# Who issues the last part of the first gate weights: SyncE in place of ScalarE, in an S5 scan with a gated GLU

## The chip, the cores and the metric

The kernel runs on one core of a Trainium2 chip. The metric is device time in microseconds (us), the median of several runs of the whole program; lower is better. A core has five engines with an instruction stream each: PE (TensorE, matmuls; PEld is its weight load), DVE (VectorE), ACT (ScalarE), POOL (GpSimd) and SP (SyncE, which here only issues DMAs). DMAs can be issued by SP, by ACT and by POOL.

## The reference, cut to what matters

```python
def _A_ref(x, Lambda_re, Lambda_im, B_re, B_im, C_re, C_im, log_dt, Dskip):
    ...
    for t in range(L):
        h = Lam_bar[None, :] * h + Bu[:, t, :]
        hs.append(h)
    hseq = jnp.stack(hs, 1)
    y = 2.0 * jnp.einsum("blp,dp->bld", hseq, Cmat).real + x * Dskip[None, None, :]
    return y

def _B_ref(x, w_gate, w_up, w_down):
    g = jnp.einsum("bsd,df->bsf", x, w_gate)
    u = jnp.einsum("bsd,df->bsf", x, w_up)
    h = _sigmoid(g) * u
    return jnp.einsum("bsf,fd->bsd", h, w_down)

x = A_x                                   # 1 x 2048 x 448, bfloat16
xn = _layernorm(x, axis=-1)
s = _A_ref(xn, ...)                       # 448 complex states
g = _silu(_B_ref(xn, B_w_gate, B_w_up, B_w_down))   # w_gate, w_up: 448 x 1792
return x + s * g
```

So every token is normalized once; the normalized token feeds a gated feed-forward block (gate, up, down) and a diagonal complex recurrence over time, and the two meet at the end.

## The kernel before, in words

The 2048 tokens are 16 tiles of 128 (tile t is rows 128t to 128t+127), and four chunks of 512 tokens. Everything that PE reads has tokens along the free axis, so a tile is normalized first and then transposed into `xnT`. Chunk 0 is transposed on PE, the later chunks by DMA.

**The order of the work** is not written out by hand engine by engine. Each step is given to a planner (`Plan`, lines 74 to 243) with an estimated cost, its reads (`r=`) and its writes (`w=`); a DMA also has a rate and, in the head of the kernel, an expected landing time (`land=`). The planner computes due times backward and a schedule forward, and the instructions are then emitted in the order of the planned starts. PE's order is fixed by a chain; DVE's and ACT's are fixed by a chain up to line 1147 and free behind it. The planner's reads order its own schedule; on the chip an instruction waits only for semaphores of work that it really depends on, and a DMA also for the landing of the DMA that used the same semaphore before it (there are eight, in turn, for the DMAs of SP and ACT together).

**The head**, up to the first dense matmul, goes like this.

- Lines 403 to 406: tile 0 is loaded by SP, tile 1 by ACT, tile 2 by SP and tile 3 by ACT, 112 KB each. Line 407: a row of parameters, by SP.
- Lines 409 to 412, `load_w0`: the first block of the gate weights (two column groups of 128, for the lower half of the hidden axis on partitions 0 to 63 and for the upper half on partitions 64 to 127), in four parts. Part A of the lower half (96 KB) by SP, part A of the upper half (128 KB) by ACT, part B of the lower half (128 KB) by SP, part B of the upper half (96 KB) by ACT.
- Lines 419 to 438: the rest of the gate weights (block 2 of 224 KB for each half, block 3 of 336 KB for each half), tiles 4 to 7, the up weights and the skip vector, all by SP, one after the other.
- Ahead of the real work PE runs ten matmuls on constants (line 444).
- Statistics of tile 0 are DVE's (line 450 `bn_stats`, line 456 `bn_aggr`), those of tile 1 are ACT's: a mean (line 488, `act_mean`), then a variance (line 492), then a root (line 496). The roots of tiles 0, 2 and 3 are ACT's too (line 484). DVE takes the reciprocals (line 481) and normalizes (line 530).
- PE transposes tile 0 (lines 568 and 570) in two groups; ACT copies the second group of slots first (line 578, "b"), then the first ("a"). Tiles 1, 2 and 3 are transposed once (lines 588, 589), copied by ACT (line 592) and shifted by DVE (line 599).
- The first two gate steps run tile by tile on PE (lines 827 and 828, function `last_tile`): for tile 0 the "b" slots, which read only parts A of the weights, then the "a" slots, which read parts B as well; then tiles 1, 2, 3. Line 827 takes the lower half of the weights, line 828 the upper half.
- From then on PE runs full 512-token steps (lines 809 and 810), first the other gate steps of chunk 0, then the seven up steps, then the projection into the states (`b_phase`, lines 883 to 900), and so on chunk by chunk to the down projections (line 1025) and the outputs (line 1044).

ACT issues its DMAs from its own instruction stream, in order with its arithmetic: what stands behind a DMA issue on ACT waits until the issue is done. Before the change, ACT's stream begins: load tile 1, load tile 3, load an activation table, issue part A of the upper half, issue part B of the upper half, `act_mean(1)`, the root of tile 0, and so on.

Of the kernel before, what the change touches and what calls it, by code (L numbers as in the profile page):

```python
# [14 lines left out]
ACT = mybir.ActivationFunctionType  # L15
# [5 lines left out]
P = 128  # L21
H = 64
# [224 lines left out]
def kernel(  # L247
# [37 lines left out]
    wsrc = {"g": B_w_gate, "u": B_w_up}  # L285
# [69 lines left out]
    def load(eng, key, nbytes, o, i, cost=0.45, r=(), rate=230e3, land=0.0):  # L355
        e = {"SP": Q, "ACT": A, "POOL": G}[eng]
        add(eng, cost, lambda: e.dma_start(out=o, in_=i), w=[key] if not isinstance(key, list) else key,  # L357
            r=r, dma=nbytes, chain=True, rate=rate).land = land
# [12 lines left out]
             wgt[k][ps, :, m0 * P:m1 * P],  # L371
             wsrc[k][:, c0 + m0 * P:c0 + m1 * P].rearrange("(s p) f -> p s f", p=H), cost=0.65, r=r, rate=rate, land=land)

    def load_w0(eng, half, part, land=0.0):
        ps = slice(half * H, half * H + H)
        s0, c0 = (1 - half if part == "A" else half), half * 896
        n = 4 - s0
        load(eng, [("w", "g", half, m, part) for m in range(2)], H * n * 2 * P * 2, wgt["g"][ps, s0:7:2, 0:2 * P],
             wsrc["g"][:, c0:c0 + 2 * P].rearrange("(s p) f -> p s f", p=H)[:, s0:7:2, :], cost=0.5, rate=400e3, land=land)

    def wkeys(k, m, part=None):
        if k == "u" or m > 1:
# [18 lines left out]
    def load_p(eng, k, r=()):  # L401
        load(eng, ("vrow", k), D * 2, vrow[k:k + 1, :], (A_log_dt, A_Lambda_im, A_Lambda_re)[k].unsqueeze(0), cost=0.75 if eng == "POOL" else 0.45, r=r)
# [4 lines left out]
    load_p("SP", 2)  # L407
    add("ACT", 0.05, lambda: A.preload_act_table_set("sqrt_and_others"), w=["sqrttab"], lat=1.3, chain=True)
    load_w0("SP", 0, "A", land=5.7)
    load_w0("ACT", 1, "A", land=5.9)  # L410
    load_w0("SP", 0, "B", land=6.9)
    load_w0("ACT", 1, "B", land=6.9)
    load_p("POOL", 0)
    load_p("POOL", 1)
    add("POOL", 0.15, lambda: G.memset(ident[:], 0.0), w=["ident"], chain=True)
# [846 lines left out]
```

## Time and profile before

| | |
|---|---|
| median of the runs | 183.85 us (3 runs: 183.84, 183.85, 184.04) |
| the profiled execution's own time | 183.57 us |
| its span, first to last instruction | 181.8 us |
| what lies around the span | 1.77 us |
| granted TensorE clock, mean by the profile's record | 1.0 |
| PE / DVE / ACT / POOL busy | 177.2 / 166.3 / 97.7 / 37.3 us |
| moved by DMA | 13.43 MB |

All times in the views are in us from the start of the span. A row of the timeline has the start, the length, the engine (SPq and ACTq are the instruction streams of SP and ACT issuing a DMA), the line in the kernel, the operation, what it writes and reads, and the count of instructions merged into the row; in brackets stands the idle time of the engine before it and what ended it. A row of the chain of waits has the start, the length and the instruction that held up the end of the kernel in this stretch. A row of the DMA issues has the size of one DMA and the time from its issue to its landing.

### The profile page before, as it was taken

The page shows a single profiled execution, that of the slowest core. Times are in us where ns is not written, and L with a number is a line of the kernel's source. Part 1 is how long each engine was busy: PE and PEld are TensorE (multiplying, and loading weights), DVE is VectorE, ACT ScalarE, POOL GpSimd, SP SyncE. Part 2 cuts the span into 40 slices and gives each one's busy share as a digit, 9 for nine tenths or more (in the row PEclk, how much of TensorE's full clock was granted, in tenths as well). Part 3 has the DMA queues.
Part 4 walks back from the last instruction along what each step waited for, and adds up shares of the span by engine and source line. Part 5 has one row for each costly group of instructions (what it writes and reads, how often), then busy time and mean ns, then how long its engine had stood idle before and what let it go on. Part 6 is the DMA issues. An engine that isn't in the chain of part 4 may idle for free.

```text
span 181.8 us, 3617 instructions
## 1 busy us (share of the span) xinstructions
PE 177.2 (97%) x1404; PEld 88.4 (49%) x1411; DVE 166.3 (91%) x295; ACT 97.7 (54%) x162; POOL 37.3 (21%) x93
## 2 busy tenths in 40 slices
PE   8999999999999999999999999999999999999993
PEld 2664445564544444445554444454555444455552
DVE  2738899999999999999999999999999999999772
ACT  4899997958799983364145543348210533411101
POOL 6352437200028998000004100000000000000000
PEclk9999999999999999999999999999999999999999
DMA  4999999999000390000004900001000000001121
GB/s 144 238 219 220 189 165 178 300 189 252 22 0 0 62 143 0 0 4 0 0 2 82 149 0 0 4 0 62 14 4 0 27 25 26 3 0 63 45 78 48
DMA packets 29956, 13.43 MB, mean 74 GB/s; under 512 B 19441, under 2 KB 29938, under 8 KB 29938
## 3 DMA queue, kind: packets, MB, share of 16 engines
q1 hardware_dynamic: 29106, 12.74, 35.0%
q10 hardware_dynamic: 768, 0.46, 1.0%
q8 instruction: 11, 0.18, 0.4%
q14 instruction: 7, 0.06, 0.1%
q0 software_dynamic: 64, 0.00, 0.0%
HBM read 6.77 MB, written 1.84 MB: 47 GB/s over the span
## 4 chain that ended last, share of the span: by engine, by line
PE 94%; DMA 1%; ACT 1%; DVE 1%; issue 1%; ACTq 0%; DVEq 0%
PE gu L809 43%; PE gu L1025 15%; PE acc L1044 11%; PE acc L1025 9%; PE gu L897 8%; PE gu L883 2%; PE acc L900 2%; PE gu L827 2%; DMA x_all<-in_A_x_dram 1%; PE acc L809 1%; PE gu L810 1%; DVE o_t L1086 0%; PE gu L828 0%; ACT junk L492 0%; ACTq L357 0%
## 5 line engine op out<-in xcount | busy, mean ns | idle before, releaser
L809 PE MATMUL gu<-xnT,wU 64*128 64x512 bf16 x196 | 45.8, 377 | 0.0
L810 PE MATMUL gu<-xnT,wU 64*128 64x512 bf16 x196 | 45.8, 376 | 0.0
L810 PE MATMUL gu<-xnT,wG 64*128 64x512 bf16 (+1 forms) x189 | 41.3, 361 | 0.0
L809 PE MATMUL gu<-xnT,wG 64*128 64x512 bf16 (+1 forms) x189 | 41.3, 361 | 0.0
L843 ACT ACTIVATE sig<-gu 128x1024 f32<-128x1024 f32 x21 | 21.3, 1021 | 25.6 <-PE gu L810 18.9
L1025 PEld LDWEIGHTS <-hF 128*128 128x128 bf16 x224 | 21.9, 98 | 20.6
L809 PEld LDWEIGHTS <-wU 64*128 64x128 bf16 x196 | 18.5, 94 | 22.8
L809 PEld LDWEIGHTS <-wG 64*128 64x128 bf16 x196 | 18.5, 94 | 19.8
L1025 PE MATMUL gu<-wd,hF 128*128 128x448 bf16 x140 | 28.0, 353 | 0.0
L846 DVE SCALAR_TENSOR_TENSOR hF<-sig,gu 128x1024 bf16<-128x1024 f32 x21 | 25.4, 1207 | 0.3
L1044 PE MATMUL acc<-cT,hT 128*128 128x448 bf16 (+2 forms) x119 | 22.9, 337 | 0.0
L964 DVE TENSOR_TENSOR_SCAN wv<-c_r,st,z 128x512 bf16<-128x512 f32 x18 | 22.9, 1275 | 0.0
L1031 ACT ACTIVATE g_t<-gu 128x448 bf16<-128x448 f32 x10 | 5.4, 539 | 27.7 <-PE gu L1025 16.8
L810 PEld LDWEIGHTS <-wU 64*128 64x128 bf16 x196 | 18.5, 94 | 0.0
L810 PEld LDWEIGHTS <-wG 64*128 64x128 bf16 x196 | 18.5, 94 | 0.0
L1025 PE MATMUL acc<-wd,hF 128*128 128x448 bf16 x84 | 16.9, 353 | 0.0
L1044 PEld LDWEIGHTS <-hT 128*128 128x128 bf16 x126 | 11.6, 98 | 9.9 <-issue 0.4
L897 PE MATMUL gu<-xnT,bT 128*128 128x512 bf16 x65 | 15.3, 380 | 0.4
L911 ACT CAST bus<-gu 128x1024 bf16<-128x1024 f32 x12 | 12.0, 1010 | 5.8 <-PE gu L883 5.3
L540 POOL COPY xn<-xn 128x448 bf16<-128x448 bf16 x12 | 7.4, 629 | 31.4 <-ACT xn L534 31.2
L917 ACT CAST bus<-acc 64x256 bf16<-64x256 f32 (+1 forms) x24 | 8.7, 368 | 5.3 <-PE acc L900 4.9
L450 DVE BATCH_NORM_STATS2 bst<-x_all 128x6 f32<-128x448 bf16 x11 | 6.4, 616 | 4.7 <-DMA x_all<-in_A_x_dram 4.7
(162 smaller groups left out, 265.6 us busy)
## 6 DMA issues: line engine op xcount, KB each, us to landing
wd<-in_B_w_down_dram SPq DMA_DIRECT2D x2, 784.0 KB, 7.5
out_dram<-o_t SPq DMA_DIRECT2D x12, 112.0 KB, 1.7
wU<-in_B_w_up_dram SPq DMA_DIRECT2D x2, 448.0 KB, 11.7
x_all<-in_A_x_dram SPq DMA_DIRECT2D x2, 448.0 KB, 4.7
wG<-in_B_w_gate_dram SPq DMA_DIRECT2D x2, 336.0 KB, 5.8
wU<-in_B_w_up_dram SPq DMA_DIRECT2D x2, 336.0 KB, 8.8
wG<-in_B_w_gate_dram SPq DMA_DIRECT2D x2, 224.0 KB, 4.7
x_all<-in_A_x_dram SPq DMA_DIRECT2D x2, 224.0 KB, 8.5
```

Source lines behind the costliest of these rows:

```text
L450: add("DVE", 0.56 if t < TPC else 0.6, lambda: V.bn_stats(out=bst[b][:], in_=x_all[:, t, :]), r=[("x", t)] + ([("xnT", 0, 3, "a")] if 3 < ...
L540: add("POOL", 0.25 if n == H else 0.6, lambda: G.tensor_copy(out=o[:, D:D + n], in_=o[:, 0:n]), r=[("xn", b)], w=[("xnw", b)])
L809: T.matmul(bank[0][:, ts], lhsT=w_[0:H, s, ms], rhs=x[0:H, SL[s], ts], start=(s == 0), stop=(s == 6))
L810: T.matmul(bank[1][:, ts], lhsT=w_[H:P, (s + 1) % 7, ms], rhs=x[H:P, SL[s], ts], start=(s == 0), stop=(s == 6))
L843: add("ACT", act(1024), lambda: A.activation(th, gu[a][:], ACT.Tanh, scale=0.5), r=[("gu", a)], w=[tk])
L846: add("DVE", dve1(1024), lambda: V.scalar_tensor_tensor(out=ho, in0=th, scalar=1.0, in1=gu[a][:], op0=ALU.add, op1=ALU.mult), r=[("gu", a) ...
L897: T.matmul(gu[slots[pt]][:, i, :], lhsT=bT[:, kt, i, pt * P:pt * P + P], rhs=x[:, kt, :], start=(first and kt == 0), stop=(not first and k ...
L911: add("ACT", act(1024), lambda: A.copy(out=bus[u][:], in_=gu[slots[pt]][:]), r=key(pt), w=[("bus", u)])
L917: add("ACT", 0.36, lambda ns=ns, d=d, q=q, l=l, i=i: A.copy(out=bus[u][d, l, ns], in_=acc[a3[i]][q, 0:256]), r=[("acc", a3[i])] + ([("bus" ...
L964: dve(1.194, lambda k=k: V.tensor_tensor_scan(out=wv[:, k, :], data0=rb, data1=z[:, k, :], initial=(st[pt][:, k, :] if c else 0.0), op0=AL ...
L1025: T.matmul(d, lhsT=hF[c % 2][:, m, h, js], rhs=wd[:, ft, :], start=(ft == 0), stop=(ft == FT - 1))
L1044: T.matmul(y, lhsT=hT[c % 2][:, hm, js], rhs=cT[:, cm, c0:c1], start=(i == 0 and not skip_on_pe), stop=(i == 6))
```

## The change

Part B of the upper half of the first gate block is issued by SP instead of ACT. `load_w0` gets a parameter `r`, passed on to `load`, and the call names tile 1's load as a read.

```diff
-    def load_w0(eng, half, part, land=0.0):
+    def load_w0(eng, half, part, r=(), land=0.0):
         ps = slice(half * H, half * H + H)
         s0, c0 = (1 - half if part == "A" else half), half * 896
         n = 4 - s0
         load(eng, [("w", "g", half, m, part) for m in range(2)], H * n * 2 * P * 2, wgt["g"][ps, s0:7:2, 0:2 * P],
-             wsrc["g"][:, c0:c0 + 2 * P].rearrange("(s p) f -> p s f", p=H)[:, s0:7:2, :], cost=0.5, rate=400e3, land=land)
+             wsrc["g"][:, c0:c0 + 2 * P].rearrange("(s p) f -> p s f", p=H)[:, s0:7:2, :], cost=0.5, r=r, rate=400e3, land=land)
...
     load_w0("SP", 0, "B", land=6.9)
-    load_w0("ACT", 1, "B", land=6.9)
+    load_w0("SP", 1, "B", r=[("x", 1)], land=6.9)
```

In the built program this DMA stands on SP right behind part B of the lower half and ahead of block 2 (line 419), and every later DMA of SP stands one place further back. It keeps the same one of the eight DMA semaphores, the one of tile 1's load, and so waits for that landing, as it did on ACT. On ACT `act_mean(1)` now follows part A directly, and carries the wait for tile 1's landing itself. PE's order stays as it was. The planner, which solves everything anew, also moves instructions on the other engines from about 17 us on: on DVE the evacuation of the second up step goes ahead of the reciprocal and the mean product of tiles 6 and 7 (lines 512, 513); on ACT the normalizations of tiles 6 and 7 (line 534) go behind one more sine table (line 686), one half of an evacuation (line 840) goes ahead of a normalization, and another sine table goes some instructions back; on POOL the copy for tile 6 (line 540) goes behind one copy of the projection weights (line 748). Around 45 to 70 us some scan, scale and statistics instructions of DVE, ACT and POOL change places with their neighbours.

## The prediction

> **What bounds the kernel now.** First the page: its span, the busy times and the shares of the chain that ended last.
>
> ```profile
> span 181.8 us, 3617 instructions
> PE 177.2 (97%) x1404; PEld 88.4 (49%) x1411; DVE 166.3 (91%) x295; ACT 97.7 (54%) x162; POOL 37.3 (21%) x93
> PE 94%; DMA 1%; ACT 1%; DVE 1%; issue 1%; ACTq 0%; DVEq 0%
> ```
>
> PE is busy for 97% of the span and carries 94% of the chain; all other engines and DMAs together hold a few per cent. So a change counts if it lets PE start its real work earlier, or makes PE wait later. Second, who PE waits for (the view of waits, PE alone):
>
> ```profile
> PE gu L444 <- PEq L1246: 0.8, 1, 0.8
> PE acc L568 <- DVE g_t L530: 0.3, 1, 0.3
> ```
>
> There are two idle stretches, both before 5.5 us. From then on PE runs on to the tail, so what the head gains or loses is handed on one for one, if no later input comes too late for an earlier PE. Third, the chain of waits in the head:
>
> ```profile
> 0.73 2.54 DMA x_all<-in_A_x_dram
> 3.27 0.02 issue
> 3.29 0.60 ACTq L357
> 3.90 0.05 issue
> 3.94 0.07 ACT junk L488
> ...
> 5.78 0.19 ACT sdb L484
> 5.96 0.39 ACT xnT L578
> 6.35 0.04 issue
> 6.40 0.21 PE gu L827
> ```
>
> Tile 1 lands at 3.27, and then ACT issues the very DMA that is moved, for 0.60 us, before its mean of tile 1 starts at 3.94. This issue is on the path.
>
> **The change, part by part.** (1) *ACT loses one issue.* The mean can start at about 3.30, 0.64 earlier. What is late next is seen in the rows of ACT, DVE and PE:
>
> ```profile
> 3.94 0.58 ACT L488 ACTIVATE junk<-x_all 128x448 bf16<-128x448 bf16 x1 [1.00 <-DMA x_all<-in_A_x_dram]
> 4.52 0.28 ACT L484 ACTIVATE sdb<-mvf,epsc 128x1 bf16<-128x1 f32 x1
> 3.79 0.18 DVE L456 BATCH_NORM_AGGREGATE mvf<-bst 128x2 f32<-128x6 f32 x1
> 3.90 0.63 DVE L450 BATCH_NORM_STATS2 bst<-x_all 128x6 f32<-128x448 bf16 x1
> 4.83 0.16 DVE L481 RECIPROCAL rsd<-sdb 128x1 f32<-128x1 bf16 x1 [0.31 <-ACT sdb L484]
> 13.35 1.16 DVE L450 BATCH_NORM_STATS2 bst<-x_all 128x6 f32<-128x448 bf16 x2 [1.53 <-DMA x_all<-in_A_x_dram]
> 0.77 4.43 PE L444 MATMUL gu<-const-bfloat16-1.0 128*128 128x512 bf16 x10 [0.77 <-PEq L1246]
> 5.49 0.51 PE L568 MATMUL acc<-ident,g_t 128*128 128x128 bf16 x6 [0.29 <-DVE g_t L530]
> ```
>
> The root of tile 0 stands behind the mean on ACT (4.52). Earlier, it meets its other input: DVE's aggregate ends at 3.97, so it starts at about 4.05 and ends at 4.33. DVE is in the statistics of tile 2 by then (from 3.90, when that tile lands). Two such instructions in a row take 1.16, so 0.53 from start to start, and the reciprocal can follow at 3.90 + 0.53 = 4.43 instead of 4.83. Behind it the aggregate of tile 2 needs those statistics (end 4.53), and the normalization follows at about 4.66 instead of 5.04. **Head: 0.38**, not 0.64. PE could take its first transposes at 5.11 instead of 5.49; its ten constant matmuls don't stop it (0.77 + 10 x 0.43 = 5.07). ACT's variance, roots and copies all hang on the same starts, so the first copy goes from 5.87 to 5.49, and the gate step from 6.40 to 6.02.
>
> (2) *PE's rate at that time.* The constant matmuls take 0.43 us each for 512 columns. Later steps take 0.22, which two rows of the up steps show:
>
> ```profile
> 22.68 0.38 PE L810 MATMUL gu<-xnT,wU 64*128 64x512 bf16 x1
> 22.89 0.38 PE L810 MATMUL gu<-xnT,wU 64*128 64x512 bf16 x1
> ```
>
> So PE runs at half rate up to some moment between its last constant matmul and 5.49, where six transposes take 0.51 with the end of the last. At half rate a transpose of 128 columns costs 0.43/4 = 0.11 instead of 0.05. If the rate rises no earlier than before, the transposes that now begin at 5.11 run slow, and the first copy, which waits for three, comes about 3 x 0.055 = 0.16 later than counted. Bounds: 0 (the rate rises before 5.11) and 0.2 or more (it rises later). I take 0.16, since 5.49 is the first time at which a row shows the full rate. Head left: 0.22.
>
> The Trainium skill says in "TensorE: Matmul & The Clock Gate", Part 1, that PE runs at half clock until a window of about 3.4 us has been busy, that the window runs freely, and that its end differs from run to run. This speaks against counting the whole 0.38; the trace agrees on the two rates (0.43 and 0.22), and no row tells when other executions switch. By it the sum would be anything from 0.55 down to 0.2.
>
> (3) *The weights' own landing.* PE's first "a" slots of tile 0 show a second, shorter hold-up, and the DMA issues show its reason.
>
> ```profile
> 7.17 0.23 PE L827 MATMUL gu<-xnT,wG 64*128 64x128 bf16 x1
> 7.34 0.23 PE L828 MATMUL gu<-xnT,wG 64*128 64x128 bf16 x1
> 2.01 1.40 SPq L357 DMA_DIRECT2D wG<-in_B_w_gate_dram  x2
> 3.53 0.60 SPq L357 DMA_DIRECT2D wG<-in_B_w_gate_dram  x1
> wG<-in_B_w_gate_dram ACTq DMA_DIRECT2D x1, 96.0 KB, 4.0
> wG<-in_B_w_gate_dram SPq DMA_DIRECT2D x1, 96.0 KB, 3.5
> wG<-in_B_w_gate_dram SPq DMA_DIRECT2D x1, 128.0 KB, 3.1
> wG<-in_B_w_gate_dram SPq DMA_DIRECT2D x1, 224.0 KB, 4.5
> ```
>
> L827 starts at 7.17, its partner L828, which reads the moved part, only at 7.34; elsewhere the two start together. The part was issued by ACT at 3.29 and landed 4.0 later, at 7.3: 0.17 of waiting. On SP the issue takes the place of block 2: SP is done with the lower part B at 3.41 (2.01 + 1.40), so it starts at 3.45. Tile 1 is there at 3.27, so the added wait costs nothing and holds nobody. Its landing is bounded by SP's own rows: 3.45 + 3.1 = 6.55 or 3.45 + 3.5 = 6.95 by the parts of its size, 7.45 if it takes ACT's 4.0, 7.95 if it takes the 4.5 of the block issued at 3.53. I take 6.8, nearest to the two parts of its size: on SP it is ahead of the 224 KB block, on ACT it shared the engines with it. PE would ask for it at 7.17 - 0.22 = 6.95, so the 0.17 goes too.
>
> (4) *SP's later DMAs* are each issued 0.62 later: an issue of 0.60 and the gap. They cost something only if they land later, and what has least room is this:
>
> ```profile
> 9.12 2.63 SPq L357 DMA_DIRECT2D wU<-in_B_w_up_dram  x2
> 13.57 8.09 SPq L394 DMA_TRANSPOSE bT<-in_A_B_re_dram  x2
> wU<-in_B_w_up_dram SPq DMA_DIRECT2D x1, 448.0 KB, 12.3
> 27.74 0.53 POOL L754 COPY bT<-bT 64x64 bf16<-64x64 bf16 x2 [0.89 <-DMA bT<-in_A_B_im_dram]
> 28.93 0.27 PE L886 MATMUL acc<-xnT,bT 64*128 64x256 bf16 x2
> ```
>
> The last up weights are the second of two issues, which starts some 0.7 behind the first, near 9.85, and lands 12.3 later, near 22.2; the rows of part (2) at 22.68 and 22.89 are the last of the step before and the first that reads them: room 0.7. POOL's copies of the projection weights end at 28.27, and PE reads them at 28.93: room 0.66, less some 0.05 for the hand-over. Both exceed what PE gains. If all landings slipped by 0.62, that room would be down to nothing, and the gain with it. I take a slip of 0: two issues of 2.63 and two of 8.09, against 0.60 for one that is not held up, show SP standing behind a full queue from 10 us on, so what paces it there is the data and not SP, and the data is the same 96 KB more or less early. The bounds are 0 and 0.62.
>
> The Trainium skill, "DMA: Bandwidth & Descriptors", section "Issuing engines are not separate DMA queues", says that DMAs from all engines share the same 16 DMA engines and that issuing from several saves only the issuing time. By that rule the landings of the later loads stay where they are and SP only pays its 0.60; no row here shows the moved DMA alone.
>
> (5) *Moved instructions behind 17 us.* PE's order is unchanged. The largest moves are those of tiles 6 and 7, whose normalization may come one sine table later (estimate 0.66: 512 columns against the 0.58 of ACT's mean over 448). Their transposes by DMA stand on SP behind issues that end only after 21.66 (13.57 + 8.09), and PE has the whole projection of chunk 0 to do, from 28.93 on, before it reads them. DVE, the next busiest, never ends a wait of PE after 5.5. I take 0, bounds -0.1 to +0.3.
>
> **Sum:** 0.38 - 0.16 + 0.17 = 0.39 earlier, against the profiled execution's 183.57: 183.18. The median stands 0.28 above that execution, with the same program; the same difference gives 183.85 - 0.39, about **183.45**.
>
> **Rivals.** *A: the part lands late on SP* (slower). It stands behind SP's own parts, and if it takes the 4.5 us of the block it displaces, it lands at 7.95, L828 starts at 7.99 instead of 7.34, and PE is 0.65 late: 184.5. It turns from gain to loss at a landing of 7.3. For it: that row of 4.5 was issued only 0.08 later. Against it: that block is more than twice as large, and two parts on SP of like size took 3.1 and 3.5.
>
> *B: SP's delay is handed on* (no change). The 0.62 arrives at the up weights and at the projection weights; PE, 0.39 earlier, waits there until about 0.05 before its old time: 183.8. For it: SP issues back to back from 2 to 9 us. Against it: the issues of 2.63 and 8.09.
>
> *C: PE's half rate eats the head.* If the rate rises well after 5.5, the transposes and small matmuls that come earlier also run slow; of a lead of 0.38 + 0.17 half is left at best, less a transpose or two: about 0.2, 183.65. For it: the median of the runs is 0.28 above the profiled execution, which a later switch could explain. Against it: that is no evidence of a switch. The page on the clock gate, named above, would call this the ordinary run-to-run case.
>
> *D: it does nothing*, because the wait that leaves ACT comes back elsewhere on it. The mean must still wait for tile 1, but that ends at 3.27; I give this no chance of its own.
>
> **Chances.** The forecast (gain 0.25 to 0.6) 0.62, A 0.13, B 0.12, C 0.13. A measurement of this kernel can tell about 0.2%, 0.37 us, from no change, and the forecast of 0.39 lies at that edge: of its 0.62, 0.48 lie beyond it (a rate that rises before 5.1 gives up to 0.55) and 0.14 short of it. Of A, 0.1 is slower by more than 0.37. So faster 0.48, same 0.41 (0.14 + 0.12 + 0.13 + 0.02), slower 0.11. The range holds the forecast with its upper bound (183.30, and 0.15 for the spread of the runs, 183.84 to 184.04), B and C: 183.15 to 184.0. A is left out.
>
> **What would show it.** ACT's L488 starts at about 3.3; the reciprocal at 4.43 and the first transpose at 5.1; the six transposes take longer than 0.51 if the half rate holds; SP's issue of 96 KB at 3.45 with 3.1 to 3.5 us to landing; L827 and L828 of tile 0's "a" slots start together near 6.95; the first 512-column step at 10.4 instead of 10.8, and the first projection matmul 0.4 before 28.93. A gap between L827 and L828 wider than 0.17 speaks for A, an earlier head with PE idle before 22.9 or 28.9 for B, a head whose 0.38 is gone by 7 us for C. The prediction is wrong if the mean starts early and PE's first transpose does not, or if PE waits anywhere after 11 us.

## The result, and the profile after

The changed kernel takes 183.54 us (median of 22 runs, 183.20 to 184.09); the kernel before, on the same chip, 183.87 (22 runs). The ratio is 0.9979, with a 95% interval of 0.9969 to 0.9988: 0.39 us faster, 0.22 to 0.57 (0.33 by the two medians). The forecast was 183.45, which is 0.39 less than before. The number came out; the steps behind it did not all.

The profiled execution of after is odd at first sight. Its own time is 183.80, longer than the 183.57 of the one before. From its page, the span and the shares of the chain of waits:

```profile
span 182.0 us, 3616 instructions
PE 85%; DMA 8%; SPq 4%; DVE 1%; issue 1%; DVEq 0%
```

Before, PE held 94% of the chain and all DMAs 1%. Now DMAs hold 8% and SP's issuing 4%: somewhere PE waited for data. The head, first, on ACT, DVE and PE (start, duration, line):

```profile
3.49 0.58 ACT L488 ACTIVATE junk<-x_all 128x448 bf16<-128x448 bf16 x1 [0.55 <-DMA x_all<-in_A_x_dram]
4.28 0.30 ACT L484 ACTIVATE sdb<-mvf,epsc 128x1 bf16<-128x1 f32 x1
4.61 0.16 DVE L481 RECIPROCAL rsd<-sdb 128x1 f32<-128x1 bf16 x1
0.77 3.63 PE L444 MATMUL gu<-const-bfloat16-1.0 128*128 128x512 bf16 x10 [0.77 <-PEq L1246]
5.26 0.51 PE L568 MATMUL acc<-ident,g_t 128*128 128x128 bf16 x6 [0.86 <-DVE g_t L530]
6.94 0.23 PE L827 MATMUL gu<-xnT,wG 64*128 64x128 bf16 x1
6.95 0.23 PE L828 MATMUL gu<-xnT,wG 64*128 64x128 bf16 x1
11.91 0.38 PE L809 MATMUL acc<-xnT,wG 64*128 64x512 bf16 x1
```

ACT's mean now follows tile 1 at once (it was 3.94), the reciprocal and the first transposes follow, and L827 and L828 start together: the moved part is there when PE asks. SP's issue and landing of that part, from the timeline of SP and the DMA issues:

```profile
3.48 0.60 SPq L357 DMA_DIRECT2D wG<-in_B_w_gate_dram  x1
wG<-in_B_w_gate_dram SPq DMA_DIRECT2D x1, 96.0 KB, 2.9
```

It lands at about 6.4. So far all is as forecast, some 0.2 later throughout, since tile 1 landed at 3.46 here instead of 3.27; only the half rate of part (2) is missing, as the six transposes take 0.51. Then comes what the forecast excluded. The chain of waits, and PE's and POOL's rows at the end of the up steps:

```profile
10.56 12.34 DMA wU<-in_B_w_up_dram
22.90 0.05 issue
22.95 0.39 PE gu L810
```

```profile
22.49 0.38 PE L809 MATMUL gu<-xnT,wU 64*128 64x512 bf16 x1
22.95 0.39 PE L810 MATMUL gu<-xnT,wU 64*128 64x512 bf16 x1
28.68 0.53 POOL L754 COPY bT<-bT 64x64 bf16<-64x64 bf16 x2 [0.28 <-DMA bT<-in_A_B_im_dram]
28.97 0.57 PE L886 MATMUL acc<-xnT,bT 64*128 64x256 bf16 x2
29.97 0.83 PE L900 MATMUL acc<-xnT,bT 128*128 128x256 bf16 x6
```

Two steps of 512 columns stand 0.21 apart; from 22.49 to 22.95 is 0.25 too much: PE waited for the last up weights, landed at 22.90. The two L886 are normally over in 0.27; here they span 0.57, because the second waits for POOL's copies of the projection weights, which end at 29.21. These are the waits that rival B foresaw; whether SP's delay brings them about is open so far. What they cost is seen in this one execution: PE was 0.40 ahead at the step of 11.91 (12.31 before) and 0.23 behind at L900 (29.74 before).

From there on the two are level: own time minus start of L900 is 153.83 for both profiled executions. **So L900's start tells the time**, and the question is what lies ahead of it.

### The profile page after: what moved, and what is told of

Read it like the earlier page. It is cut to its first block, busy times and chain, and to the rows that moved or that the text cites. A ratio compares the mean times of both kernels' runs of the same rounds, so it can differ in the third digit from the quotient of the medians.

```text
span 182.0 us, 3616 instructions
## 1 busy us (share of the span) xinstructions
PE 176.8 (97%) x1404; PEld 88.1 (48%) x1411; DVE 165.9 (91%) x295; ACT 98.1 (54%) x162; POOL 35.1 (19%) x93
## 4 chain that ended last, share of the span: by engine, by line
PE 85%; DMA 8%; SPq 4%; DVE 1%; issue 1%; DVEq 0%
PE gu L809 34%; PE gu L1025 15%; PE acc L1044 11%; PE acc L1025 9%; PE gu L897 8%; DMA wU<-in_B_w_up_dram 7%; PE gu L810 4%; SPq L357 4%; PE gu L883 2%; PE acc L900 2%; DMA x_all<-in_A_x_dram 1%; DVE o_t L1086 0%; PE acc L886 0%; DVE o_t L1080 0%; PE acc L1042 0%
## 5 line engine op out<-in xcount | busy, mean ns | idle before, releaser
L809 PE MATMUL gu<-xnT,wU 64*128 64x512 bf16 x196 | 46.0, 376 | 0.0
L809 PE MATMUL gu<-xnT,wG 64*128 64x512 bf16 (+1 forms) x189 | 41.3, 360 | 0.0
L809 PEld LDWEIGHTS <-wG 64*128 64x128 bf16 x196 | 18.4, 94 | 19.9
L809 PEld LDWEIGHTS <-wU 64*128 64x128 bf16 x196 | 18.3, 94 | 19.6
L1044 PE MATMUL acc<-cT,hT 128*128 128x448 bf16 (+2 forms) x119 | 22.9, 337 | 0.0
L964 DVE TENSOR_TENSOR_SCAN wv<-c_r,st,z 128x512 bf16<-128x512 f32 x18 | 22.9, 1276 | 0.0
L810 PEld LDWEIGHTS <-wU 64*128 64x128 bf16 x196 | 18.3, 94 | 3.7 <-DMA wU<-in_B_w_up_dram 0.6
L540 POOL COPY xn<-xn 128x448 bf16<-128x448 bf16 x12 | 8.2, 690 | 28.5 <-ACT xn L534 28.4
```

The source lines that it names most:

```text
L540: add("POOL", 0.25 if n == H else 0.6, lambda: G.tensor_copy(out=o[:, D:D + n], in_=o[:, 0:n]), r=[("xn", b)], w=[("xnw", b)])
L809: T.matmul(bank[0][:, ts], lhsT=w_[0:H, s, ms], rhs=x[0:H, SL[s], ts], start=(s == 0), stop=(s == 6))
L810: T.matmul(bank[1][:, ts], lhsT=w_[H:P, (s + 1) % 7, ms], rhs=x[H:P, SL[s], ts], start=(s == 0), stop=(s == 6))
L964: dve(1.194, lambda k=k: V.tensor_tensor_scan(out=wv[:, k, :], data0=rb, data1=z[:, k, :], initial=(st[pt][:, k, :] if c else 0.0), op0=AL ...
L1044: T.matmul(y, lhsT=hT[c % 2][:, hm, js], rhs=cT[:, cm, c0:c1], start=(i == 0 and not skip_on_pe), stop=(i == 6))
```

## The experiments

Theory T: the head gains 0.4 to 0.5 (ACT's issue off the path, the part in time), and part of that lead is lost again where PE meets SP's later loads. Rivals: R1, only the part's landing pays; R2, nothing is given back and the late loads of that execution are chance.

**More executions of both kernels.** No edit.

> The changed kernel once more, for a second execution. Theory T (the head gains 0.4 to 0.5, and SP's later landings, some 0.6 later, give part of it back): first 512-column step at 10.3 to 10.4, the last up weights land at 22.8 to 23.0 and the last projection weights at 28.2 to 28.6, PE waits for both, and the time is 0.2 to 0.45 below that of the kernel before. Rival R2 (those landings were chance in one execution): up weights at 22.2, projection weights at 27.6, no wait of PE behind 11 us, 0.4 to 0.5 below.

> The changed kernel a third time, for its profile. T: last up weights at 22.8 to 22.9 as in the two others, PE waits for them and for the projection weights; the two-core-microsecond stretch from 6 to 8 us moves less than the 273 GB/s of the kernel before. R2: an execution that is free of late landings turns up, with the last up weights at 22.2.

> The kernel before once more, for a second profile. T (the late landings come with the change: between 5.5 and 8 us the DMA engines run short of issued bytes, and what is missing stays missing): 190 to 240 GB/s or more in all the half microseconds from 6 us on, last up weights at 22.0 to 22.3, projection weights at 27.5 to 27.7, PE waits for neither. R2 (the landings vary by chance from execution to execution): somewhere between 22.0 and 23.0.

> The kernel before a third time, for its profile. T: the moved part, issued by ACT at 3.3 to 3.5, lands at 7.2 to 7.8, later than PE asks for it (7.0 to 7.2), and the projection starts without a wait, so PE's time to the projection is set by the head alone: 16.62 from the first step of the second block column of chunk 0 to the projection, as in the two other profiles.

The rows that carry the reading, first of the second and third profile of the kernel before:

```profile
5.65 0.51 PE L568 MATMUL acc<-ident,g_t 128*128 128x128 bf16 x6 [1.03 <-DVE g_t L530]
7.33 0.23 PE L827 MATMUL gu<-xnT,wG 64*128 64x128 bf16 x1
7.82 0.23 PE L828 MATMUL gu<-xnT,wG 64*128 64x128 bf16 x1 [0.26 <-DMA wG<-in_B_w_gate_dram]
```

```profile
7.37 0.23 PE L827 MATMUL gu<-xnT,wG 64*128 64x128 bf16 x1
7.66 0.23 PE L828 MATMUL gu<-xnT,wG 64*128 64x128 bf16 x1
29.02 0.53 POOL L754 COPY bT<-bT 64x64 bf16<-64x64 bf16 x2 [0.15 <-DMA bT<-in_A_B_im_dram]
29.31 0.57 PE L886 MATMUL acc<-xnT,bT 64*128 64x256 bf16 x2
```

then of the second of after, which met late up weights (two steps stand 0.38 apart instead of 0.21):

```profile
22.48 0.38 PE L810 MATMUL gu<-xnT,wU 64*128 64x512 bf16 x1
22.86 0.39 PE L810 MATMUL gu<-xnT,wU 64*128 64x512 bf16 x1
```

and of the third of after, which met no late up weights but late projection weights:

```profile
22.47 0.38 PE L809 MATMUL gu<-xnT,wU 64*128 64x512 bf16 x1
22.68 0.38 PE L809 MATMUL gu<-xnT,wU 64*128 64x512 bf16 x1
28.29 0.53 POOL L754 COPY bT<-bT 64x64 bf16<-64x64 bf16 x2 [0.75 <-DMA bT<-in_A_B_im_dram]
28.58 0.57 PE L886 MATMUL acc<-xnT,bT 64*128 64x256 bf16 x2
```

All six profiled executions, each with its own time ("stage" is from the first 512-column step into acc, L809, to L900; with no wait in it, it takes 17.25 to 17.28, as in the second of before and in three kernels below):

| | ACT's mean L488 | transposes L568 | L828 behind L827 | step L809 acc | stage | POOL's last copies L754 | L900 | time |
|---|---|---|---|---|---|---|---|---|
| before | 3.94 | 5.49 | 0.17 | 12.31 | 17.43 | 27.74 | 29.74 | 183.57 |
| before, 2nd | 4.11 | 5.65 | 0.49 | 12.79 | 17.28 | 27.24 | 30.07 | 183.92 |
| before, 3rd | 4.14 | 5.68 | 0.29 | 12.62 | 17.63 | 29.02 | 30.25 | 184.09 |
| after | 3.49 | 5.26 | 0.01 | 11.91 | 18.06 | 28.68 | 29.97 | 183.80 |
| after, 2nd | 3.35 | 5.12 | 0.00 | 11.77 | 18.12 | 28.51 | 29.89 | 183.72 |
| after, 3rd | 3.47 | 5.24 | 0.00 | 11.89 | 17.63 | 28.29 | 29.52 | 183.36 |

Means of three: transposes 0.40 earlier; the wait for the part 0.31 less; the step at 12 us 0.72 earlier (12.57 against 11.86), the sum of the two. The stage is 0.49 longer, and L900 is 0.23 earlier, as is the time (183.86 against 183.63). R2 has its point too: before's third execution also met late loads, where T forecast none, and after's third no late up weights, where T forecast them. Three profiles of each are few, and those of the change may overstate what is lost: the first two lie 0.26 and 0.35 above the medians of their timings (the second is the slowest of its 12), while the first of before lies 0.28 below the median that it was recorded with. The second profile of after brought a second timing as well: ratio 0.9978 (0.9962 to 0.9995).

**The part by ACT, without the second issue.** The kernel before, with the upper half's parts in one load:

```diff
-    load_w0("ACT", 1, "A", land=5.9)
+    load("ACT", [("w", "g", 1, m, q) for m in range(2) for q in "AB"], ...)   # 7 slots, 224 KB
-    load_w0("ACT", 1, "B", land=6.9)
```

> The upper half's two parts go out as one ACT load of 224 KB; no second issue on ACT, and SP issues as in the kernel before. T: ACT's mean of tile 1 right behind the landing (3.3 to 3.5), the block lands by 6.2 to 6.6, the first 512-column step at 10.3 to 10.4, SP's later landings as in the kernel before (up weights 22.2, projection weights 27.6), so nothing is given back: 0.45 to 0.55 below the kernel before, some 0.1 better than the change. R1 (only the part's landing pays, not ACT's free issue slot): at most 0.17 below. R2 (nothing was given back by the change either): level with the change, 0.35 below.

```profile
5.15 0.51 PE L568 MATMUL acc<-ident,g_t 128*128 128x128 bf16 x6 [0.27 <-DVE g_t L530]
6.06 0.21 PE L827 MATMUL gu<-xnT,wG 64*128 64x128 bf16 x1
6.27 0.23 PE L828 MATMUL gu<-xnT,wG 64*128 64x128 bf16 x1
```

The transposes come as early as with the change, so it is ACT's issue that made them late: as an account of the head, R1 falls. The block lands at 6.2 and holds the first slot up by 0.2. The stage is 17.27: nothing is lost behind it. But this profiled execution, at 183.21, is the fastest of its 12; the median is 183.49, and the ratio 0.9992 (0.9981 to 1.0004). That is some 0.15 us, where T forecast 0.45 to 0.55 and R1 at most 0.17. By its time the run doesn't speak for T, and one profile doesn't tell why.

**SP late, with nothing to carry.** The kernel before, with a small load (0.8 KB by the page) on SP ahead of block 2:

```diff
+    scr = sbt("scr", [3, 2])
+    load("SP", ("scr",), H * 3 * 4, scr[0:H, :, :], ..., cost=0.5, r=[("x", 1)], rate=400e3)
```

> The kernel before, with one more issue on SP ahead of the third gate block: a load of 1.5 KB to a scratch tile that nobody reads. SP's later issues come 0.6 later with no bytes added; ACT issues the part as before. T: the last up weights land at 22.7 to 22.9 and the projection weights at 28.1 to 28.5; since PE has no lead here, it costs only what exceeds the room of 0.7 and 0.66: 0 to 0.15 above the kernel before. R2 (the data sets the pace, not the issue): landings at 22.2 and 27.6 as before, 0.

```profile
5.49 0.55 PE L571 MATMUL acc<-ident,g_t 128*128 128x128 bf16 x6 [0.29 <-DVE g_t L533]
7.20 0.23 PE L830 MATMUL gu<-xnT,wG 64*128 64x128 bf16 x1
7.21 0.23 PE L831 MATMUL gu<-xnT,wG 64*128 64x128 bf16 x1
wG<-in_B_w_gate_dram ACTq DMA_DIRECT2D x1, 96.0 KB, 3.4
```

(Lines are 3 higher here.) Block 2 goes out at 4.20, as with the change, yet the last up weights land at about 22.0 and POOL's last copies start at 27.67: in this execution a later SP made nothing late. And an unplanned finding: ACT's part, issued at 3.28 as before, now lands 3.4 later instead of 4.0 to 4.3, in time for PE. So ACT's queue alone doesn't make it slow, and block 2, issued beside it before, is a likely reason; this is one profile, and two others further down don't fit so simple a rule. Ratio 1.0002 (0.9989 to 1.0014), as both theories allowed. Own time minus start of L903 (L900 in the others) is 154.11 here, 0.28 more than in the first two profiles, so this execution's time doesn't tell what its head was worth.

**The part by ACT, at once.** The kernel before, with the third parameter row on POOL; that leaves a semaphore free, and ACT issues the part at 2.44, without waiting for tile 1:

```diff
-    load_p("SP", 2)
     ...
     load_p("POOL", 1)
+    load_p("POOL", 2)
```

> The kernel before, with the third parameter row issued by POOL instead of SP, which frees a semaphore: ACT issues the moved part right behind its first one, from 2.4 to 3.0, ahead of tile 1's landing, and SP has one issue less. T: ACT's mean of tile 1 at 3.3 to 3.5, the part lands at 6.5 to 6.9, the first 512-column step at 10.3 to 10.4, SP's later landings 0.3 to 0.4 earlier than in the kernel before, no wait of PE behind 11 us: 0.45 to 0.55 below the kernel before. R1 (only the part's landing pays): 0.17 below. R2 (SP's place costs nothing): level with the change, 0.35 below.

ACT's mean starts at 3.38 and the transposes at 5.15, but the parameter row lands at 6.06 instead of early, and PE's little transposes, which stand ahead of the gate steps, wait for it:

```profile
6.19 0.21 PE L634 MATMUL acc<-ident,hF 3*128 3x3 bf16 x3 [0.48 <-DMA hF<-in_A_Lambda_re_dram]
```

The step L809 acc is at 12.20, 0.34 behind the change. All the same the ratio is 0.9984 (0.9972 to 0.9997): 0.29 us, where T forecast 0.45 to 0.55, R1 0.17 and R2 0.35; the interval separates none of the three. The profiled execution is the slowest of its 12 (183.83 against a median of 183.46), and T's forecast that PE meets no wait behind 11 us is a miss in it:

```profile
28.68 0.53 POOL L754 COPY bT<-bT 64x64 bf16<-64x64 bf16 x2 [0.23 <-DMA bT<-in_A_B_im_dram]
28.97 0.57 PE L886 MATMUL acc<-xnT,bT 64*128 64x256 bf16 x2
```

SP issues one DMA less than before here, and block 2 goes out at 3.66 (before: 3.53). The projection weights are late all the same, as late as in the first profile of the change, and PE loses 0.13 at the up weights as well (steps at 22.77 and 23.11). So these waits also come without the change's delay of SP.

**Up weights earlier.** The load of tiles 6 and 7 behind the last two up weights, once with the change and once without:

```diff
-    load_x(6, 2, land=19.3)
-    load_w("SP", "u", 0, 1, rate=400e3, land=20.9)
-    load_w("SP", "u", 1, 1, rate=400e3, land=22.5)
+    load_w("SP", "u", 0, 1, rate=400e3, land=19.8)
+    load_w("SP", "u", 1, 1, rate=400e3, land=21.4)
+    load_x(6, 2, land=22.5)
```

> The change, with the load of tiles 6 and 7 moved on SP from ahead of the last two up-weight loads to behind them. These land about 1 us earlier. T (PE gives part of its lead back at the up weights): the wait at the up weights goes; what is left is that for the projection weights, so the gain over the change is 0 to 0.1, and no more, unless these come earlier too. R2 (nothing is given back): level with the change, 0.2% below the kernel before.

> The same move in the kernel before, where PE waits neither for the up weights nor for the projection weights: no gain, level with the kernel before within 0.1%, by both theories. A loss would be the price of tiles 6 and 7 coming later, to be taken off the run with the change.

With the change 0.9984 (0.9973 to 0.9995), no gain over it; without it 1.0033 (1.0022 to 1.0043). The control failed: the same move costs 0.6 us in the kernel before and nothing with the change, and no run shows why, so the pair tells nothing about the up weights. (The profile without the change is that kernel's slowest execution, 185.69 against a median of 184.30, and isn't read.) But the profile with the change shows rival C at work:

```profile
0.77 4.42 PE L444 MATMUL gu<-const-bfloat16-1.0 128*128 128x512 bf16 x10 [0.77 <-PEq L1246]
5.19 0.82 PE L568 MATMUL acc<-ident,g_t 128*128 128x128 bf16 x6
```

Six transposes in 0.82 instead of 0.51: PE was still at half rate, and L809 acc comes at 12.08.

**SP's place given back.** The change, with the lower half's parts in one load, so that block 2 goes out at 3.54 again:

```diff
-    load_w0("SP", 0, "A", land=5.7)
+    load("SP", [("w", "g", 0, m, q) for m in range(2) for q in "AB"], ...)   # 7 slots, 224 KB
     load_w0("ACT", 1, "A", land=5.9)
-    load_w0("SP", 0, "B", land=6.9)
-    load_w0("SP", 1, "B", r=[("x", 1)], land=6.9)
+    load_w0("SP", 1, "B", land=6.9)
```

> The change, with the two parts of the lower half (128 and 96 KB on SP) in one load of 224 KB. SP has one issue less, so block 2 is issued at 3.5 again instead of 4.2, and the moved part at 2.8, without a wait for tile 1. The order on PE, DVE and ACT is that of the change. T2 (the late projection weights come from the DMA engines being short of issued bytes between 5.5 and 8 us, since block 2 goes out 0.65 later): 235 GB/s or more in that stretch, the last projection weights at 27.0 to 27.6, no wait of PE there; the merged block lands at 6.2 to 6.6, so the head is 0.1 to 0.4 later than with the change; time 0.1 above to 0.3 below the change. R3 (SP's place is not the reason): weights at 28.2 to 28.6 as in the three profiles of the change, and the time 0.1 to 0.4 above the change.

```profile
5.14 0.51 PE L568 MATMUL acc<-ident,g_t 128*128 128x128 bf16 x6 [0.48 <-DVE g_t L530]
6.65 0.23 PE L827 MATMUL gu<-xnT,wG 64*128 64x128 bf16 x1 [0.67 <-DMA wG<-in_B_w_gate_dram]
12.39 0.38 PE L809 MATMUL acc<-xnT,wG 64*128 64x512 bf16 x1
29.65 0.83 PE L900 MATMUL acc<-xnT,bT 128*128 128x256 bf16 x6
```

PE waits 0.67 for the merged block, and its lead at 12 us is all but gone (12.39, where the change has 11.86 and before 12.57). And yet the ratio is 0.9979 (0.9961 to 0.9998), the change's own: the stage takes 17.26 and L900 is at 29.65, close to the change's mean of 29.79. **In this execution, half a microsecond less of lead at 12 us is not seen again at L900.** POOL's last copies start at 27.91, between the forecasts of T2 and R3. T2's forecast about bytes was missed: from 5.5 to 8 us the DMA engines moved 215 GB/s, not 235 or more. Windows of before, after and this kernel (the last two columns are the DMA engines' share and GB/s):

```profile
5.50:8.00 2.50, 2.43 (x46) 1.92 (x47) 2.13 (x9) 2.18 (x7) 0.98 (x2) 1.00 1.03 246
```

```profile
5.50:8.00 2.50, 2.43 (x51) 1.94 (x48) 2.11 (x10) 2.02 (x8) 0.98 (x2) 1.00 0.78 197
```

```profile
5.50:8.00 2.50, 1.83 (x42) 1.32 (x40) 1.68 (x8) 1.72 (x6) 1.05 (x1) 1.00 0.96 215
```

The first two rows alone would mislead: the three profiles of the change have 197, 217 and 230 in this stretch, the three of before 246, 237 and 217.

**Projection weights earlier.** The change, with the skip vector's load (112 KB) behind them on SP, run twice:

```diff
-    load("SP", "dbc", ..., rate=400e3, land=22.7)
     ...
     b_load()
+    load("SP", "dbc", ..., rate=400e3, land=27.8)
```

> The change, with the load of the skip vector (114 KB) moved on SP from ahead of the projection weights to behind them. T (PE's start of the projection waits 0.35 to 0.7 for these weights): they land 0.2 to 0.6 earlier, at 27.6 to 28.2, and the time falls by 0.1 to 0.4 below the change, to 0.3 to 0.4% below the kernel before. R2 (nothing given back there on average): level with the change within 0.1.

> The change with the skip vector behind the projection weights once more: its first profile was the slowest of its 12 executions (184.05 against a median of 183.27). T (the lead is lost at the projection weights, and these come earlier here): 0.3 to 0.4% below the kernel before, the last projection weights at 27.3 to 27.7, and PE starts the projection with a wait of at most 0.2. R2 (no help; the first run was luck): 0.2% below the kernel before, as the change, and a wait of 0.35 or more.

Ratios 0.9968 (0.9950 to 0.9985) and 0.9971 (0.9951 to 0.9991), medians 183.27 and 183.35, about what T forecast. The second profile:

```profile
5.14 0.82 PE L568 MATMUL acc<-ident,g_t 128*128 128x128 bf16 x6
18.07 0.38 PE L809 MATMUL gu<-xnT,wU 64*128 64x512 bf16 x1
18.53 0.39 PE L809 MATMUL gu<-xnT,wU 64*128 64x512 bf16 x1
27.66 0.53 POOL L754 COPY bT<-bT 64x64 bf16<-64x64 bf16 x2
28.90 0.27 PE L886 MATMUL acc<-xnT,bT 64*128 64x256 bf16 x1
```

POOL's copies are done at 28.19, 0.7 before PE's first L886: that wait is gone. Another is left, 0.25 for the first block of up weights at 18.3, and 0.3 of its stage is a gap in PE's weight loads at L883 for which the profile shows no releaser. Both executions also had PE's late half rate, and both were the slowest of their 12 (184.05 and 183.70), so the profiles show less than the medians. Against the change itself the intervals overlap: a further 0.1 to 0.2 is likely and not separated.

## Why the prediction was right, and where it was not

- **(1) The head, 0.38: right.** 0.40 by the means of three, and the kernel that only spares ACT the second issue shows the transposes at 5.15 too. The times of that kernel and of the one with the parameter row on POOL (0.15 and 0.29 us) don't separate this from R1; the rows of the head do. What limits it is as told: L484 at 4.28, not at 3.5, and the reciprocal behind it on DVE.
- **(2) PE's half rate, 0.16: right in size, not always there.** None of the three profiles of the change has it, so there the term was 0. In 3 of the 9 profiles in which ACT doesn't issue the part late, the transposes run at half rate (0.73 to 0.82 for six) and L809 acc comes at 11.99 to 12.08; in the three of the change it is at 11.77 to 11.91. The price is 0.18. The ten constant matmuls take 4.42 or 4.43 in those, none of them fast, and 3.63 to 4.12 in the others, so the rise itself moves: from about 3.5 us ((4.43 - 3.63) / 0.21, some four of the ten at the short duration) to beyond 5.7. That the moment differs from run to run agrees with the Trainium skill, "TensorE: Matmul & The Clock Gate", Part 1; the spread of 500 ns either way that it gives there is narrower than the 2.2 us or more seen here.
- **(3) The part's landing, 0.17: mis-sized.** In before it cost 0.17, 0.49 and 0.29, mean 0.31. I took it from one execution, in which tile 1, for which ACT's issue waits, landed earliest. The part came 4.0 to 4.3 after its issue on ACT, and 2.9 to 3.1 on SP, with the change. Rival A's fear, a late landing on SP, had no ground: never later than about 6.6 in the three profiles.
- **(4) SP's later DMAs, 0: the step that failed.** "Both exceed what PE gains" were the words, and the rooms of 0.7 and 0.66 came from one execution. At the projection weights the two others of before have a room of 1.64 (copies done at 27.77, read at 29.41) and none. In all three profiles of the change PE waits for the projection weights, in two for up weights, and the stage is 0.38 to 0.87 over its least of 17.25 (before: 0.03 to 0.38). So these waits took 0.49 of a lead of 0.72, where the term was put at 0, and by the prediction's own sign ("if PE waits anywhere after 11 us") the mechanism was wrong here. Rival B foresaw the waits, but its reason for them, SP's 0.62 handed on, is not shown (below).
- **(5) Reorders, 0.** No row spoke against it: own time minus L900 stayed at 153.83 to 153.85 in all six, and POOL's last copies wait for their DMA in all three profiles of the change (0.28 to 0.75), not for a moved instruction.

So the sum of 0.39 was 0.40 + 0.31 - 0.49 = 0.22 in these profiles, and 0.33 by the medians of either timing. Against the forecast (2) gave 0.16 more, (3) 0.14 more and (4) 0.49 less; that these misses cancel as far as they do, and the number came out, is luck. The median of before stood 0.28 above its profiled execution, and that profile has the best head of three; that the median belongs to executions that wait longer for the part is likely, but not shown.

What stays open is why the loads come later. POOL's last copies start at 28.29 to 28.68 with the change, at 27.24 and 27.74 in two of three before, which would fit SP's 0.62. But three things speak against SP's place as the main reason. First, the delay fades on SP itself: block 2 goes out 0.66 later in all three profiles of the change, the last up weights 0.33 later (10.43 against 10.10, means of three) and the first projection weights no later at all. Here are the issues of these in the third profile of before and the third of the change:

```profile
14.10 8.35 SPq L394 DMA_TRANSPOSE bT<-in_A_B_re_dram  x2
13.37 8.63 SPq L394 DMA_TRANSPOSE bT<-in_A_B_re_dram  x2
```

The others are at 13.57 and 14.10 before, at 14.14 and 13.66 with the change. That is what the prediction meant by the data setting the pace. And the last up weights land at about 22.2, 22.3 and 23.2 before and at 22.9, 22.9 and 22.2 with the change, hardly later by the means. Second, with SP as late and nothing else moved the copies start at 27.67. Third, they start at 28.68 where only the parameter row is moved to POOL, and at 29.02 in before's third, both without the delay on SP. Over 4 to 20 us the DMA engines moved 228, 224 and 214 GB/s in the three profiles of before and 213, 223 and 225 in those of the change, and the two lowest of the six go with the two latest copies. So chance from execution to execution is a large part of it, and the share that is due to SP isn't settled. What is shown is the other half: part of PE's lead is lost where it meets such a landing, since the landings did not come earlier when PE did.

## What to carry to other kernels

A lead that is won in the head is worth what the tightest later landing lets through: list the loads behind the change with the room of each, and compare that room with the lead. Take the room from several executions, since one profile showed 0.66 where another had none. And when one engine's issue of a DMA stands ahead of its arithmetic on the path, its cost is not the 0.6 us of the issue but the distance to the next input, here 0.40.

## What the runs showed of the hardware that was not expected

- The same program's loads vary more than its time: the last copies of the projection weights started at 27.24, 27.74 and 29.02 in three executions of the kernel before, whose times are 183.57 to 184.09.
- The landing of a 96 KB part is not set by the engine that issues it alone: it came 4.0 to 4.3 us after an issue by ACT with a 224 KB block issued within 0.25 on SP (three profiles; 3.8 in that of the control with tiles 6 and 7 moved), 3.4 by ACT with that block 0.9 later, 2.9 to 3.5 on SP ahead of it (six profiles). The Trainium skill, "DMA: Bandwidth & Descriptors", section "Issuing engines are not separate DMA queues", has DMAs of all engines share the same 16 DMA engines, and these rows agree. A later block isn't enough for a short landing, though: it took 4.4 by ACT issued at 2.44 with that block 1.2 later, and 4.2 on SP issued at 2.81 with it 0.7 later (one profile each), so what went out just before may count as well.
